# Softmax sums of a causal attention turned on the vector engine instead of sent through DMA, with the first loads in one row

## The chip, the cores and the metric

One core of a Trainium2 chip. The metric is device time in microseconds (us) of one execution. Engines are named as in the profile: PE (TensorE matmul), PEld (its weight load), DVE (VectorE), ACT (ScalarE), POOL (GpSimd), SP (SyncE, which here only issues DMAs).

## The reference

Two stages, both in float32 for the reader, in 16-bit matmuls in the kernel. Attention over B = 8 batches, H = 8 heads, S = 576 queries, D = 64, with 16 beacon keys that every query sees ahead of the causal ones; then an MLP over all 4608 tokens (512 to 2048 to 512) with a quick-GELU gate:

```python
scores = scale * np.matmul(q, concat(beacon_k, k).T)      # 576 x 592
scores = np.where(causal, -1e9, scores)
a = np.exp(scores - scores.max(-1)); a /= a.sum(-1) + 1e-09
x = np.matmul(a, concat(beacon_v, v))                     # then heads side by side: 4608 x 512
h = x @ w_in
out = (h / (1 + np.exp(-1.702 * h))) @ w_out
```

## The kernel before, in words

**Steps.** The attention runs in 32 steps, one for each batch b and pair of heads p (step i = 4b + p). A step computes the scores of both heads in four chunks (L352, PE, into `s`, two PSUM buffers), exponentiates each (L365, ACT, into `E`), masks the triangles on the diagonal in place (L381 on DVE with a mask tile `keep`, or L388 on POOL), and multiplies with v (L422, PE). v stands in a tile `vb` beside 64 columns of ones, so that the output `u` of a head x and half of the queries (128 rows x 288 columns, one PSUM buffer) holds the unnormalised result in 64 rows and the softmax sum, repeated, in the other 64. For x = 0 the result is in rows 0 to 63, for x = 1 in rows 64 to 127. 18 matmuls of L422 make the four outputs of a step.

**PSUM.** `u` is a ring of four buffers which everything else shares: the turned q, k and v of the first two batches (L178, L215), the L422 outputs, and both MLP layers. PE waits when the fourth buffer back has not been read.

**Normalising.** Each `u` is copied whole to an SBUF tile `O` (L436, an eviction, on ACT or DVE). Two pairs (half a batch, hf) share one `O`. In batches 2 to 7 the sums of two pairs are gathered by two DMAs into a small tile `zc`, DVE takes the reciprocal (`rc`, L455), a DMA writes it to DRAM (`zd`), two DMAs spread it over 64 partitions each (`rz`, 288 KB), and four multiplications of 64 rows (a norm, L500, on DVE or POOL) write `xT`, the MLP's input. In batches 0 and 1 (`TZ = 2`) no DMA is used: DVE transposes the 32 x 32 squares of the sums from `O` (`zt`, L478), takes the reciprocal of one column in 32 (`rt`, L486), and transposes that back, repeated 32 times (`rz`, L491).

**MLP.** Nine groups of 512 tokens; for each, 16 first-layer units (L528, 4 matmuls of 512 columns; tanh on ACT, L539; gate on DVE, L544, into `g`) and four second-layer units (L559, 16 matmuls; halved on ACT or DVE, L570; stored by SP). An L528 unit needs the norms of its batches, so the MLP runs beside later attention steps, and the rest behind the last.

**q and k.** The first two batches come in by POOL's DMAs (L150, L160) and are turned on PE; later batches are loaded to `n` (L132), turned by DVE in squares (L276), reordered by DVE or POOL (L285), written to DRAM and placed (SP).

**What sets the order.** Every piece of work is entered in a list as a `Work` with an engine (or a choice of engines), an estimated duration, a key (a due time in steps) and what it needs. A planner, `issue()`, goes through the list once while the program is built: it takes what could start first, by its estimates, and among those the smallest key. The order that comes out is fixed on each engine; at run time each engine follows its row and waits by semaphores. `MLP0` and `PACE` set the keys of the MLP units. A DMA issued by POOL waits for the one eight issues earlier (`DMASW0` to `DMASW7` are these eight lanes).

Of the kernel before, what the change touches and what calls it, by code (L numbers as in the profile page):

```python
# [10 lines left out]
F32 = mybir.dt.float32  # L11
AFT = mybir.ActivationFunctionType
ALU = mybir.AluOpType
# [3 lines left out]
def kernel(  # L17
# [37 lines left out]
    MLP0, PACE = 6.5, 7  # L55
    FILL, FILLT = 150, 60.0
    VMASK = 8
    TZ = 2
# [7 lines left out]
    op_ = ctx.enter_context(tc.tile_pool(name="op", bufs=2))  # L66
# [363 lines left out]
    def av_out(i, x, half, eng):  # L430
        b, p = divmod(i, NPAIR)
        if (b, p // 2) not in Os:
            Os[(b, p // 2)] = [
                op_.tile([P, 2, S], F32, tag=f"O{y}", name=f"O{y}") for y in range(2)
            ]
        copy[eng](  # L436
            out=Os[(b, p // 2)][x][:, p % 2, half * HS : (half + 1) * HS],
            in_=avu[(i, x, half)][:, :],
        )

# [3 lines left out]
    def z_gather(b, hf, y):  # L444
        if y == 0:
            zst[(b, hf)] = [zp.tile([64, 36], F32, tag="zc", name="zc")]
        src = (Os[(b, hf)][0][D : D + 1, :, :], Os[(b, hf)][1][0:1, :, :])[y]
        nc.sync.dma_start(
            out=zst[(b, hf)][0][32 * y : 32 * y + 32, :],
            in_=src.rearrange("o a s -> o (a s)"),  # L450
        )

    def z_recip(b, hf):
        rc = zp.tile([64, 36], F32, tag="rc", name="rc")
        nc.vector.reciprocal(out=rc[:, :], in_=zst[(b, hf)][0][:, :])  # L455
        zst[(b, hf)].append(rc)

    def z_write(b, hf):
        zd = dr.tile([2, 2 * S], F32, tag="zd", name="zd")
        nc.sync.dma_start(out=zd.rearrange("y (r c) -> (y r) c", c=36), in_=zst[(b, hf)][1][:, :])  # L460
        zst[(b, hf)].append(zd)

    def z_spread(b, hf, y):
        if y == 0:
            zst[(b, hf)].append(zp.tile([P, 2, S], F32, tag="rz", name="rz"))
        nc.sync.dma_start(  # L466
            out=zst[(b, hf)][3][64 * y : 64 * y + 64, :, :].rearrange("r a s -> r (a s)"),
            in_=zst[(b, hf)][2][y : y + 1, :].to_broadcast([64, 2 * S]),
        )

    zts = {}

    def z_turn(b, hf, a, y):
        if (a, y) == (0, 0):
            zts[(b, hf)] = zp.tile([P, 2, TPP, SQ], F32, tag="zt", name="zt", bufs=1)
        nc.vector.transpose(  # L478
            zts[(b, hf)][64 * y : 64 * y + 64, a, :, :],
            Os[(b, hf)][y][64 * (1 - y) : 64 * (1 - y) + 64, a, :],  # L480
        )

    def z_turn_recip(b, hf, a):
        if a == 0:
            zst[(b, hf)] = [None, None, zp.tile([P, 2, TPP], F32, tag="rt", name="rt", bufs=1)]
        nc.vector.reciprocal(out=zst[(b, hf)][2][:, a, :], in_=zts[(b, hf)][:, a, :, 0])  # L486

    def z_turn_back(b, hf, a):
        if a == 0:
            zst[(b, hf)].append(zp.tile([P, 2, S], F32, tag="rz", name="rz"))  # L490
        nc.vector.transpose(  # L491
            zst[(b, hf)][3][:, a, :],
            zst[(b, hf)][2][:, a, :].unsqueeze(2).to_broadcast([P, TPP, SQ]),
        )

    def norm(b, hf, n, eng):
        c = (b % RING) * S
        a, y = divmod(n, 2)
        r = 64 * y
        vec[eng].tensor_tensor(  # L500
            out=xT[r : r + 64, 2 * hf + a, c : c + S],
            in0=Os[(b, hf)][y][r : r + 64, a, :],
            in1=zst[(b, hf)][3][r : r + 64, a, :],
            op=ALU.mult,
        )
# [88 lines left out]
    class Buf:  # L594
# [5 lines left out]
        n0=2, n1=2, sq=2, t0=2, t1=2, d0=4, d1=4, qT=2, kT=2, vb=2, s=2, E=2, u=4, O=2,  # L600
        zc=2, rc=2, zd=4, rz=2, zt=1, rt=1, xT=RING, sig=3, g=2, osb=3,
# [15 lines left out]
    last = []  # L617

    def first_loads(b):
        k0 = 4 * b - 3  # L620
        gb6 = Buf("g")
        lds = {}
        for g in range(2):
            for w in (1, 0):
                lds[(g, w)] = Work(
                    "POOL", 0.9, k0 - 2 + 0.1 * g, lambda b=b, g=g, w=w: load_qk6(b, g, w),
                    last[:], alloc=gb6 if not lds else None, dma=1.8, after=list(lds.values())[:1],
                )
# [126 lines left out]
    for i in range(NSTEP):  # L755
# [33 lines left out]
        if p % 2 == 0:  # L789
            Ob = Buf("O")  # L790
            evs = {}
        for x in range(2):
            for half in range(2):
# [12 lines left out]
                ev = Work(  # L806
                    dict(DVE=0.44, ACT=0.45), 0, i + 0.5,
                    lambda eng, i=i, x=x, half=half: av_out(i, x, half, eng), [av],
                    alloc=Ob if not evs else None, after=list(evs.values())[:1],
                )  # L810
                use(u_, ev)
                evs[(p, x, half)] = ev
        if b < TZ:
            if p % 2 == 0:
                zb = [Buf("zt"), Buf("rt"), Buf("rz")]
            a = p % 2
            zn = []
            for y in range(2):
                zn.append(Work(
                    "DVE", 0.68, i + 0.45, lambda b=b, hf=hf, a=a, y=y: z_turn(b, hf, a, y),  # L820
                    [e for (pp, x, half), e in evs.items() if (pp, x) == (p, y)],
                    alloc=zb[0] if (a, y) == (0, 0) else None, after=zn[:1],
                ))
            zr = Work(
                "DVE", 0.2, i + 0.45, lambda b=b, hf=hf, a=a: z_turn_recip(b, hf, a), zn,
                alloc=zb[1] if a == 0 else None,
            )
            zk = Work(
                "DVE", 0.68, i + 0.45, lambda b=b, hf=hf, a=a: z_turn_back(b, hf, a), [zr],
                alloc=zb[2] if a == 0 else None,  # L830
            )
            use(zb[0], *zn, zr)
            use(zb[1], zr, zk)
            use(Ob, *zn)
            for y in range(2):
                n = 2 * a + y
                nw = Work(
                    dict(DVE=0.76, POOL=1.42), 0, i + 0.45,
                    lambda eng, b=b, hf=hf, n=n: norm(b, hf, n, eng), [zk],
                    alloc=xTb[b] if (hf, n) == (0, 0) else None,  # L840
                    after=[norms[(b, 0, 0)]] if (hf, n) != (0, 0) else (),
                )
                norms[(b, hf, n)] = nw
                use(Ob, nw)
                use(zb[2], nw)
# [189 lines left out]
```

## Time and profile before

| | us |
|---|---|
| median of 3 runs | 435.76 (432.81 to 437.97) |
| the profiled execution | 430.96 |
| its span in the profile | 429.1 |
| PE busy | 381.3 (89%) |
| DVE busy | 262.5 (61%) |
| ACT busy | 235.0 (55%) |
| POOL busy | 170.3 (40%) |

The profile is of one execution; its span is what the trace covers, and the 1.9 us beside it lie around the program. A busy PE need not be a fast one: the granted clock (PEclk, 1.00 is full) halves in some stretches. A row of the view of waits names the instruction that waited, then what released it, with the total, the number of times and the longest. In a row of the timeline the bracket holds the idle time ahead of the instruction and what ended it.

### The profile page before, as it was taken

To read this page: it belongs to the slowest core of one execution; us is meant where nothing else is said; L and a number is where in the kernel's file an instruction comes from. 1 tells how busy PE (TensorE), PEld (TensorE's weight loads), DVE (VectorE), ACT (ScalarE), POOL (GpSimd) and SP (SyncE) were. 2 spreads that over 40 slices of the span, in tenths; PEclk is the share of its full clock that TensorE was granted. 3 is DMA by queue.
4 is the path that set the end of the run, shared out by engine and by line. 5 is a ranking of instruction groups with operands and counts; after the bars stand their busy time and mean duration, and the time that the engine had idled before them with its cause. 6 is when DMAs were issued, how large, how long until landed. Compare 5 with 4: busy or idle time off the path is not lost. (4 is left out here: it accounts for less than half of the span.)

```text
span 429.1 us, 6682 instructions
## 1 busy us (share of the span) xinstructions
PE 381.3 (89%) x2459; PEld 188.6 (44%) x2459; DVE 262.5 (61%) x441; ACT 235.0 (55%) x391; POOL 170.3 (40%) x253
## 2 busy tenths in 40 slices
PE   7997777989885988897969898949999999999996
PEld 3454433444442434343434565624445444444442
DVE  5479989699466296826877499353664544534310
ACT  1787766767452458544826666625666353444411
POOL 6458755376246255644438268132332010000000
PEclk9999969899997999698999999979999999999999
DMA  9899996696679727895449759732202031010111
GB/s 119 116 152 200 172 198 123 165 83 157 162 179 165 196 79 177 83 158 156 116 134 145 186 119 151 160 98 80 81 28 82 26 105 49 24 49 26 50 50 73
DMA packets 64929, 50.13 MB, mean 117 GB/s; under 512 B 34689, under 2 KB 55681, under 8 KB 64897
## 3 DMA queue, kind: packets, MB, share of 16 engines
q0 software_dynamic: 42816, 18.62, 38.3%
q1 hardware_dynamic: 22080, 31.10, 24.0%
q8 instruction: 19, 0.31, 0.3%
q14 instruction: 14, 0.11, 0.1%
HBM read 51.48 MB, written 16.72 MB: 159 GB/s over the span
## 5 line engine op out<-in xcount | busy, mean ns | idle before, releaser
L528 PE MATMUL u<-xT,w 128*128 128x512 f16 (+1 forms) x640 | 145.9, 375 | 17.7 <-DVE xT L500 8.3
L559 PE MATMUL u<-w,g 128*128 128x512 f16 x576 | 132.3, 385 | 4.3 <-DVE O L436 4.3
L544 DVE SCALAR_TENSOR_TENSOR g<-sig,u 128x512 f16<-128x512 f16 x144 | 96.1, 679 | 59.0 <-ACT sig L539 57.7
L539 ACT ACTIVATE sig<-u 128x512 f16<-128x512 f32 x144 | 85.9, 602 | 53.3 <-PE u L528 48.7
L365 ACT ACTIVATE E<-s 128x1024 f16<-128x1024 f32 (+3 forms) x128 | 107.0, 872 | 6.5 <-PE s L352 4.0
L528 PEld LDWEIGHTS <-w 128*128 128x128 f16 x640 | 61.0, 101 | 82.5 <-issue 24.8
L388 POOL TENSOR_SCALAR_AFFINE_SELECT E<-E 128x256 f16<-128x256 f16 (+2 forms) x120 | 52.3, 448 | 108.0 <-ACT E L365 106.4
L559 PEld LDWEIGHTS <-g 128*128 128x128 f16 x576 | 56.1, 99 | 72.4 <-issue 9.0
L570 ACT ACTIVATE osb<-u 128x512 f32<-128x512 f32 x36 | 21.5, 597 | 104.0 <-PE u L559 104.0
L422 PE MATMUL u<-E,vb 128*128 128x288 f16 (+6 forms) x576 | 61.0, 248 | 4.3 <-DVE g L544 3.0
L422 PEld LDWEIGHTS <-vb 128*128 128x128 f16 (+1 forms) x576 | 45.0, 99 | 26.3 <-issue 13.3
L500 DVE TENSOR_TENSOR xT<-O,rz 64x576 f16<-64x576 f32 x48 | 45.0, 953 | 18.8 <-DMA rz<-zd 18.4
L352 PE MATMUL s<-qT,kT 64*128 64x80 f16 (+5 forms) x384 | 38.3, 290 | 14.3 <-ACT E L365 6.2
L436 DVE COPY O<-u 128x288 f32<-128x288 f32 x63 | 27.2, 446 | 31.4 <-PE u L422 29.1
L285 POOL COPY t<-sq 128x576 f16<-128x576 f16 x25 | 32.6, 1312 | 31.2 <-DVE sq L276 31.2
L276 DVE STREAM_TRANSPOSE sq<-n 128x576 f16<-128x576 f16 x48 | 34.7, 750 | 7.8 <-DMA n<-in_k_dram 7.7
L500 POOL TENSOR_TENSOR xT<-O,rz 64x576 f16<-64x576 f32 x16 | 25.9, 1619 | 33.3 <-DMA rz<-zd 31.9
L436 ACT COPY O<-u 128x288 f32<-128x288 f32 x65 | 25.2, 404 | 14.8 <-PE u L422 12.4
L352 PEld LDWEIGHTS <-kT 64*128 64x128 f16 x384 | 13.6, 95 | 38.3 <-issue 30.8
L244 POOL DMA_DIRECT2D vb<-in_v_dram x24 | 20.7, 867 | 0.1
L285 DVE COPY t<-sq 128x576 f16<-128x576 f16 x23 | 17.2, 760 | 0.2
L381 DVE TENSOR_TENSOR E<-E,keep 128x256 f16<-128x256 f16 (+2 forms) x40 | 13.6, 366 | 4.9 <-ACT E L365 3.1
(48 smaller groups left out, 135.5 us busy)
## 6 DMA issues: line engine op xcount, KB each, us to landing
out_dram<-osb SPq DMA_DIRECT2D x36, 256.0 KB
rz<-zd SPq DMA_DIRECT2D x24, 288.0 KB
d<-t SPq DMA_DIRECT2D x24, 148.0 KB
kT<-d SPq DMA_DIRECT2D x12, 296.0 KB
n<-in_k_dram POOLq DMA_DIRECT2D x12, 288.0 KB, 6.9
n<-in_q_dram POOLq DMA_DIRECT2D x12, 288.0 KB, 8.1
d<-t SPq DMA_DIRECT2D x24, 144.0 KB
qT<-d SPq DMA_DIRECT2D x12, 288.0 KB
```

The source lines that it names most:

```text
L276: nc.vector.transpose(sqs[(b, g, w)][:, c * n : (c + 1) * n, :, :], nat[(b, g, w)][:, c * n : (c + 1) * n, :],)
L285: copy[eng](out=tqk[(b, g, w)][:, e, o : o + S].rearrange("p (r t) -> p r t", t=TPP), in_=sqs[(b, g, w)][:, :, e, :].rearrange("p t r -> p ...
L352: nc.tensor.matmul(sc[:, x, o : o + e - a], kT[r : r + 64, p, j * P : (j + 1) * P], qT[r : r + 64, p, a:e], start=True, stop=True,)
L365: nc.scalar.activation(out=Es[i][:, :, choff[ci] : choff[ci] + w], in_=scs[(i, ci)][:, :, 0:w], func=AFT.Exp, scale=0.125,)
L388: nc.gpsimd.affine_select(out=blk, in_=blk, compare_op=ALU.is_ge, fill=0.0, base=mc, pattern=[[0, 2], [1, w]], channel_multiplier=-1,)
L422: nc.tensor.matmul(u[:, lo:hi], vb[0:kw, j, :, :].rearrange("r h c -> r (h c)")[:, o : o + 2 * D], E[0:kw, x, col : col + hi - lo], start= ...
L436: copy[eng](out=Os[(b, p // 2)][x][:, p % 2, half * HS : (half + 1) * HS], in_=avu[(i, x, half)][:, :],)
L500: vec[eng].tensor_tensor(out=xT[r : r + 64, 2 * hf + a, c : c + S], in0=Os[(b, hf)][y][r : r + 64, a, :], in1=zst[(b, hf)][3][r : r + 64, ...
L528: nc.tensor.matmul(u[:, o : o + w], w1t[:, kp, nt * P : (nt + 1) * P], xT[:, kp, m : m + w], start=(kp == 0), stop=(kp == NKP - 1),)
L539: nc.scalar.activation(out=sig[:, :], in_=hu[(g, nt)][:, :], func=AFT.Tanh, scale=0.851)
L544: nc.vector.scalar_tensor_tensor(out=gts[g][:, nt, :], in0=hs[(g, nt)][:, :], scalar=1.0, in1=hu[(g, nt)][:, :], op0=ALU.add, op1=ALU.mult,)
L559: nc.tensor.matmul(o[:, :], gts[g][:, nt, mt * P : (mt + 1) * P], w2t[:, nt, :], start=(nt == 0), stop=(nt == NNT - 1),)
```

## The change

All batches now normalise without DMA, one pair at a time. For each of the four `u` of a step DVE transposes the squares of the 64 rows of sums straight out of PSUM (`z_turn`, 64 x 288), and only the other 64 rows are evicted (`av_out`). When the four turns of a pair are there, one reciprocal, one turn back and one multiplication of 128 rows follow. `O` now holds one pair, in three buffers. The planner may give the multiplication to POOL, but the order has all 32 on DVE. `MLP0` is 4.6 for 6.5. The loads of batch 1, and `w_in`, no longer need the v load before them, their due times are all ahead of the first step, and the `w_out` quarters need less.

```diff
-    MLP0, PACE = 6.5, 7
+    MLP0, PACE = 4.6, 7
-    TZ = 2
-    op_ = ctx.enter_context(tc.tile_pool(name="op", bufs=2))
+    op_ = ctx.enter_context(tc.tile_pool(name="op", bufs=3))
...
     def av_out(i, x, half, eng):
+        if i not in Os:
+            Os[i] = op_.tile([P, S], F32, tag="O", name="O")
+        r = 64 * x
+        copy[eng](
+            out=Os[i][r : r + 64, half * HS : (half + 1) * HS],
+            in_=avu[(i, x, half)][r : r + 64, :],
+        )
+    def z_turn(i, x, half):
+        if i not in zst:
+            zst[i] = [zp.tile([P, TPP, SQ], F32, tag="zt", name="zt")]
+        n = HS // SQ
+        nc.vector.transpose(
+            zst[i][0][64 * x : 64 * x + 64, half * n : (half + 1) * n, :],
+            avu[(i, x, half)][64 * (1 - x) : 64 * (1 - x) + 64, :],
+        )
+    def z_recip(i):
+        zst[i].append(zp.tile([P, TPP], F32, tag="rt", name="rt"))
+        nc.vector.reciprocal(out=zst[i][1][:, :], in_=zst[i][0][:, :, 0])
+    def z_back(i):
+        zst[i].append(zp.tile([P, S], F32, tag="rz", name="rz"))
+        nc.vector.transpose(
+            zst[i][2][:, :],
+            zst[i][1][:, :].unsqueeze(2).to_broadcast([P, TPP, SQ]),
+        )
+    def norm(i, eng):
+        b, p = divmod(i, NPAIR)
         c = (b % RING) * S
         vec[eng].tensor_tensor(
+            out=xT[:, p, c : c + S], in0=Os[i][:, :], in1=zst[i][2][:, :], op=ALU.mult
         )
...
     def first_loads(b):
-        k0 = 4 * b - 3
+        k0 = 4 * b
+        kl = -5 + 0.4 * b
...
-                    "POOL", 0.9, k0 - 2 + 0.1 * g, lambda b=b, g=g, w=w: load_qk6(b, g, w),
-                    last[:], alloc=gb6 if not lds else None, dma=1.8, after=list(lds.values())[:1],
+                    "POOL", 0.7, kl + 0.1 * g, lambda b=b, g=g, w=w: load_qk6(b, g, w),
+                    alloc=gb6 if not lds else None, dma=1.8, after=list(lds.values())[:1],
...
-        W1.append(Work("POOL", 1.1, 4.1 + 0.01 * c, lambda c=c: load_w1(c), last[:], dma=3.0))
-        W2.append(Work("POOL", 1.1, 4.2 + 0.01 * c, lambda c=c: load_w2(c), vpe[:], dma=3.0))
+        W1.append(Work("POOL", 0.75, -4 + 0.01 * c, lambda c=c: load_w1(c), dma=3.0))
...
+                zn.append(Work(
+                    "DVE", 0.4, i + 0.48, lambda i=i, x=x, half=half: z_turn(i, x, half), [av],
+                    alloc=zb[0] if not zn else None, after=zn[:1],
+                ))
...
+        zr = Work("DVE", 0.2, i + 0.45, lambda i=i: z_recip(i), zn, alloc=zb[1])
+        zk = Work("DVE", 0.75, i + 0.45, lambda i=i: z_back(i), [zr], alloc=zb[2])
+        nw = Work(
+            dict(DVE=0.78, POOL=1.45), 0, i + 0.45, lambda eng, i=i: norm(i, eng), [zk] + evs,
+            alloc=xTb[b] if p == 0 else None, after=[norms[b * NPAIR]] if p else (),
+        )
```

What this does to the order, at three places. The first is DVE's row in the middle of the program, before, around step 16 counted from 0; `rc<-zc` is the reciprocal, `g<-sig,u` a gate, `sq` and `t` the turning of q and k, `O<-u` an eviction, `xT<-O,rz` a norm:

```order
L381 TENSOR_TENSOR E<-E,keep 128x2x128 [waits Activation_49]
L381 TENSOR_TENSOR E<-E,keep 128x2x80
L455 RECIPROCAL rc<-zc 64x36 [waits DMAHW1_49,DMAHW0_49]
L544 SCALAR_TENSOR_TENSOR g<-sig,u 128x512 [waits Activation_49]
L291 STREAM_TRANSPOSE t_2205<-bk 128x2x32
L276 STREAM_TRANSPOSE sq<-n_2116 128x576
L285 COPY t_2299<-sq 128x576 [waits DMAHW6_49,DMAHW5_49,DVE_49]
L436 COPY O_2219<-u 128x288 [waits PE_49] x2
L436 COPY O_2220<-u 128x288 [waits PE_49]
L500 TENSOR_TENSOR xT<-O_1964,rz 64x576 [waits DMAHW0_49]
L500 TENSOR_TENSOR xT<-O_1965,rz 64x576 [waits DMAHW1_49]
L500 TENSOR_TENSOR xT<-O_1965,rz 64x576
```

The same engine at about the same place, with the change; `zt<-u` is a turn out of PSUM, `rz<-rt` the turn back:

```order
L447 STREAM_TRANSPOSE zt<-u 64x288 [waits PE_49] x4
L507 SCALAR_TENSOR_TENSOR g<-sig,u 128x512 [waits Activation_49]
L454 RECIPROCAL rt<-zt 128x18 [waits DVE_49]
L458 STREAM_TRANSPOSE rz<-rt 128x576 [waits DVE_49]
L507 SCALAR_TENSOR_TENSOR g<-sig,u 128x512 [waits Activation_49]
L466 TENSOR_TENSOR xT<-O,rz 128x576 [waits DVE_49]
L507 SCALAR_TENSOR_TENSOR g<-sig,u 128x512 [waits Activation_49] x2
L275 STREAM_TRANSPOSE sq<-n_2473 128x576 [waits DMASW0_49]
L275 STREAM_TRANSPOSE sq<-n_2473 128x576
```

The reciprocal and the norms no longer wait for DMAs of SP (`DMAHW`), and follow the turns of their own pair; before, the norms of steps 14 and 15 stood behind evictions of step 16 and waited there.

The second place is ACT's row around there, before; `E<-s` is an exp, `sig<-u` a tanh:

```order
L436 COPY O_1964<-u 128x288 [waits PE_49]
L539 ACTIVATE sig<-u 128x512 [waits DVE_49]
L539 ACTIVATE sig<-u 128x512 [waits DVE_49,PE_49]
L365 ACTIVATE E<-s 128x2x464 [waits PE_49]
L436 COPY O_1964<-u 128x288 [waits PE_49]
L365 ACTIVATE E<-s 128x2x208
L436 COPY O_1965<-u 128x288 [waits PE_49] x2
```

And with the change:

```order
L502 ACTIVATE sig<-u 128x512 [waits DVE_49,PE_49]
L533 ACTIVATE osb<-u 128x512 [waits DMAHW3_49,PE_49]
L364 ACTIVATE E<-s 128x2x512 [waits PE_49,Pool_49]
L433 COPY O<-u 64x288 [waits DVE_49] x3
L364 ACTIVATE E<-s 128x2x480
```

An eviction used to wait for PE alone; here three wait for DVE's turns of the same `u`. Of ACT's 114 evictions (65 before) 72 stand so; at the other 42 the turn waits for ACT.

The third place is POOL's row at the start, before; `g` are q and k of the first batches, `w_99<-in_v_dram` their v:

```order
L150 DMA g<-in_q_dram 96x4x384
L160 DMA w_99<-in_v_dram 96x8x384
L99 AFFINE_SELECT spread<-spread 96x648 [waits DVE_49]
L87 AFFINE_SELECT keep<-keep 128x144
L388 AFFINE_SELECT E<-E 128x2x112 [waits Activation_49]
L388 AFFINE_SELECT E<-E 128x2x128 [waits Activation_49]
L388 AFFINE_SELECT E<-E 128x2x80
L388 AFFINE_SELECT E<-E 128x2x128 [waits Activation_49] x2
L150 DMA g<-in_k_dram 96x4x384
L150 DMA g<-in_q_dram 96x4x384 [waits DMASW0_49]
```

With the change, from the second load of batch 1 on:

```order
L149 DMA g<-in_q_dram 96x4x384 [waits DMASW0_49]
L149 DMA g<-in_k_dram 96x4x384 [waits DMASW1_49]
L149 DMA g<-in_q_dram 96x4x384 [waits DMASW2_49]
L159 DMA w_99<-in_v_dram 96x8x384 [waits DMASW3_49]
L98 AFFINE_SELECT spread<-spread 96x648 [waits DVE_49]
L250 DMA w_98<-in_moe_w_in_dram 128x4x512 [waits DMASW4_49]
L250 DMA w_98<-in_moe_w_in_dram 128x4x512 [waits DMASW5_49]
L250 DMA w_98<-in_moe_w_in_dram 128x4x512 [waits DMASW6_49]
L250 DMA w_98<-in_moe_w_in_dram 128x4x512 [waits DMASW7_49]
L86 AFFINE_SELECT keep<-keep 128x144
L257 DMA w_99<-in_moe_w_out_dram 128x4x512 [waits DMASW0_49]
L387 AFFINE_SELECT E<-E 128x2x112 [waits Activation_49]
```

The masks of the first step (`E<-E`) moved behind batch 1's loads, all of `w_in` and a quarter of `w_out`; each of these DMAs waits for an earlier one to land before it is issued.

More of the change, by code (lines that the diff above doesn't have):

```diff
@@ L473 @@
[L473 to L486, printed above, removed]
@@ L878 @@
+        norms[i] = nw
+        use(zb[0], zr)
+        use(zb[1], zk)
+        use(zb[2], nw)
+        use(Ob, nw)
     for w, i in late:
```

135 lines of the change are left out of this document (15 added, 120 removed).

## The prediction

> **What bounds the kernel now.** First the page: who is busy, and for how much of the span.
>
> ```profile
> span 429.1 us, 6682 instructions
> PE 381.3 (89%) x2459; PEld 188.6 (44%) x2459; DVE 262.5 (61%) x441; ACT 235.0 (55%) x391; POOL 170.3 (40%) x253
> ```
>
> PE bounds it, but a mean over stages hides where it loses time. I cut the span where a step's last L422 matmul ends (18 a step): step 8 of 32 ends at 82.1, step 32 at 335.7. The view by windows (columns: length, busy time of each engine, granted clock, DMA share, GB/s):
>
> ```profile
> core 0: us, PE busy (x) PEld busy (x) DVE busy (x) ACT busy (x) POOL busy (x), PEclk, DMA share, GB/s
> 10.00:82.10 72.10, 59.33 (x563) 31.80 (x558) 57.24 (x97) 52.30 (x88) 43.12 (x70) 0.93 1.03 160
> 82.10:335.50 253.40, 224.49 (x1456) 113.23 (x1455) 164.89 (x286) 145.74 (x243) 119.36 (x167) 0.95 0.68 129
> 82.10:101.60 19.50, 17.91 (x118) 8.88 (x117) 18.94 (x34) 14.64 (x27) 12.51 (x19) 1.00 0.91 136
> 200.00:220.00 20.00, 19.84 (x127) 9.68 (x126) 16.13 (x28) 13.31 (x23) 9.46 (x13) 0.93 0.42 103
> 335.70:425.60 89.90, 89.81 (x417) 40.51 (x414) 34.40 (x51) 34.85 (x60) 1.39 (x1) 1.00 0.15 51
> ```
>
> The tail after 335.7 is pure matmul at full clock: nothing to win there. The 24 steps of 82.1 to 335.5 lose 253.4 - 224.5 = 28.9 us to waits of PE and, at a mean clock of 0.95, 0.05 x 253.4 = 12.7 us to a slow clock; unhindered they would be 211.8 us. The view of waits says whom PE waited for there:
>
> ```profile
> PE u L528 <- DVE xT L500: 8.3, 5, 5.5
> PE u L528 <- DVE O L436: 5.4, 2, 4.0
> PE u L559 <- DVE O L436: 4.3, 1, 4.3
> PE u L528 <- DVE g L544: 3.4, 3, 2.1
> ...
> DVE xT L500 <- DMA rz<-zd: 18.4, 9, 6.6
> DVE rc L455 <- DMA zc<-O: 11.2, 4, 6.3
> ```
>
> PE names DVE, and DVE, from its own waits, names the two DMAs of the softmax sums. The timeline shows both as one event, and the chain of waits has it at its head too:
>
> ```profile
> 131.04 0.75 DVE L500 TENSOR_TENSOR xT<-O,rz 64x576 f16<-64x576 f32 x1 [2.77 <-DMA rz<-zd]
> 135.06 1.47 DVE L436 COPY O<-u 128x288 f32<-128x288 f32 x4
> 135.50 1.01 PE L559 MATMUL u<-w,g 128*128 128x512 f16 x2 [4.32 <-DVE O L436]
> 172.97 1.44 PE L528 MATMUL u<-xT,w 128*128 128x512 f16 x3 [2.07 <-DVE g L544]
> 275.41 8.34 DMA rz<-zd
> ```
>
> DVE stood at a norm (L500) whose broadcast had not landed; the evictions behind it in DVE's queue (L436) came late, and PE, which needed a `u` buffer that one of them held, stood 4.32 us. So DVE, idle in a third of these steps, bounds PE by what it waits for. Behind such waits the clock drops; the seventh number is the clock:
>
> ```profile
> 134.60:141.40 6.80, 5.90 (x14) 2.02 (x14) 3.97 (x9) 0.00 (x0) 3.60 (x6) 0.50 1.11 143
> 172.20:178.90 6.70, 5.93 (x17) 2.06 (x16) 5.84 (x9) 1.75 (x5) 4.24 (x6) 0.50 0.31 66
> ```
>
> Each wait thus costs itself and half of some 6.8 us. The Trainium skill (TensorE: Matmul & The Clock Gate, HAM oscillation) asks for no idle gap over about 3.4 us; the trace is stricter, since the 2.07 us at 172.97 stood at a half clock as well. By that rule only waits over 3.4 us would carry the surcharge, and a crowd of new waits of 1 us would cost no more than their own length.
>
> **The change part by part.**
>
> *The chain of sums without DMA.* Per pair of heads: four turns out of PSUM, one reciprocal, one turn back, one norm of 128 rows. In the 24 steps the DMA waits go, and PE's 8.3 + 5.4 + 4.3 with them, and the 3.4 of gates that stood behind norms: 21.4 us, and the 12.7 us of clock. On SP 60 issues go (24 zc, 12 zd, 24 rz), which the writes of q and k no longer queue behind. Late next is DVE itself, for the work moves there. Its rows, and one of ACT, from the 24 steps (count, busy us, mean ns, idle before), and from L478 on from the whole run:
>
> ```profile
> L500 DVE TENSOR_TENSOR xT<-O,rz 64x576 f16<-64x576 f32 x31 | 29.7, 977 | 18.7 <-DMA rz<-zd 18.4
> L436 DVE COPY O<-u 128x288 f32<-128x288 f32 x54 | 23.3, 447 | 28.7 <-PE u L422 26.6 <-issue 1.8
> L455 DVE RECIPROCAL rc<-zc 64x36 f32<-64x36 f32 x11 | 4.0, 363 | 11.2 <-DMA zc<-O 11.2
> L381 DVE TENSOR_TENSOR E<-E,keep 128x256 f16<-128x256 f16 x17 | 6.2, 367 | 1.1 <-ACT E L365 1.0
> L276 DVE STREAM_TRANSPOSE sq<-n 128x576 f16<-128x576 f16 x40 | 28.9, 749 | 7.7 <-DMA n<-in_k_dram 7.7
> ...
> L436 ACT COPY O<-u 128x288 f32<-128x288 f32 x41 | 15.9, 404 | 8.6 <-PE u L422 6.4 <-POOL xT L500 1.2 <-POOL E L388 0.7
> L478 DVE STREAM_TRANSPOSE zt<-O 64x576 f32<-64x576 f32 x16 | 12.4, 773 | 2.6 <-ACT O L436 2.1
> L491 DVE STREAM_TRANSPOSE rz<-rt 128x576 f32<-128x576 f32 x8 | 6.2, 769 | 0.1
> L486 DVE RECIPROCAL rt<-zt 128x18 f32<-128x18 f32 x8 | 2.0, 247 | 0.0
> L500 DVE TENSOR_TENSOR xT<-O,rz x48: 718/756/1907, 29.5 to 355.7; 64x576 f16<-64x576 f32 x48
> ```
>
> Added: 96 turns out of PSUM, a form that no trace shows. A copy of the same 288 columns out of PSUM takes 0.447 (L436), a turn of 576 columns from SBUF 0.773 (L478). Ends: 0.39, half of 0.773, if all of a turn goes by columns, and 0.773 if none does; I take 0.47, close to the copy, which shares source and length. 96 x 0.47 = 45.1 (37.4 to 74.2). 24 reciprocals x 0.247 = 5.9. 24 turns back x 0.769 = 18.5. 24 norms, twice the rows but the same 576 columns, now all on DVE: 0.82, between the median 0.756 and the mean 0.977, since POOL's norms go: 19.7. Together 89.2. Gates, by the order, 92 for 89: +2.0. Removed: 29.7; 23.3 less 12 evictions that stay (5.4); 4.0; 17 masks that the order gives to POOL (17 x 0.37 = 6.3); 5 turns of q and k that it puts ahead of step 8 (3.7): 61.6. DVE goes from 164.9 to 194.5 us (187 to 224). Against the 211.8 us of PE that is 92%: **DVE becomes nearly as full as PE.**
>
> The longest norm took 1907 ns, and POOL gets 143 masks for 120. The Trainium skill (SBUF — State Buffer, Who interferes with whom) says that a DVE instruction with two SBUF inputs, as a norm is, contends with POOL instructions that read SBUF, and one with at most one such input does not. By that rule norms stay at the mean of 0.977, and DVE's sum is 24 x 0.157 = 3.8 us higher, 400 in place of 396 below if all of it reached PE; the turns out of PSUM are spared. By the rows it lies between.
>
> *What that does to PE* the windows show. With DVE at 81% (16.13 of 20) PE was busy 19.84 of 20. With DVE at 97% (18.94 of 19.5) PE was 8% idle. I take 7% on 211.8: 226 us, where DVE stands at 86%, between these rows. Ends: none (212), and 17% (248), twice the 8% of the fuller row, when the turn is at its high end (DVE 224 us, 90% of 248).
>
> *A wait added.* In the order an ACT eviction of `u` waits for the DVE turn of the same buffer, or the turn for the eviction. Queued behind such an eviction on ACT are exps and tanhs, for which PE and DVE wait. ACT has room: 145.7 of 253.4 us busy, and some 41 evictions more at 0.404 make 162. Where four turns stand in a row with the evictions after them, ACT lags by one of them a step, which the 7% holds; what it costs when PE pays for every one is a rival below.
>
> *The loads in one row.* POOL issues 12 loads before `spread`, then `w_in` and one `w_out` load, and the first masks stand behind all.
>
> ```profile
> 4.89 0.67 POOL L150 DMA_DIRECT2D g<-in_q_dram  x1
> 5.55 0.78 POOL L160 DMA_DIRECT2D w<-in_v_dram  x1
> 12.82 0.38 POOL L388 TENSOR_SCALAR_AFFINE_SELECT E<-E 128x224 f16<-128x224 f16 x1 [5.50 <-ACT E L365]
> 16.33 6.65 PE L215 MATMUL u<-w,spread 96*128 96x512 f16 x30
> 23.68 1.75 PE L422 MATMUL u<-E,vb 128*128 128x288 f16 x18
> g<-in_q_dram POOLq DMA_DIRECT2D x4, 288.0 KB, 6.2
> w<-in_v_dram POOLq DMA_DIRECT2D x2, 576.0 KB, 9.2
> ```
>
> Its last lane waits for batch 1's first q load. The last q of batch 0 (4.89 + 6.2) landed at about 11.1, v behind it (5.55 + 9.2) at about 14.8, so 576 KB took some 3.7 us; k and q of batch 1, 288 KB each, land as much later, near 18.5; three masks like this one end at about 20. PE needs them at 23.68: its 6.65 us of v matmuls hide the delay, and I cost it at nothing; without that cover it is up to 7 us, the shift of the masks. What arrives earlier (batch 1, `w_in`) nobody waited for by the rows above, so no gain either.
>
> *More MLP earlier.* Counted in the order, steps 1 to 8 get 3 more L528 groups and 2 of L559: 9.5 us of PE work that leaves the tail, where 37 and 14 groups stay of 44 and 15.
>
> ```profile
> L559 PE MATMUL u<-w,g 128*128 128x512 f16 x240 | 53.4, 379 | 0.0
> L528 PE MATMUL u<-xT,w 128*128 128x512 f16 x176 | 39.6, 379 | 0.0
> ```
>
> The tail's 59 groups of 89.9 us are 15 x 16 + 44 x 4 = 416 matmuls of 0.216; 372 remain: 80.4 us. In the first stretch PE had 72.1 - 59.3 = 12.8 us idle and 0.07 x 72.1 = 5 us of clock, and DVE's work is about the same, so most of the 9.5 us fits: I put step 8's end at 84, 91 if none of it is hidden, 79 if a quarter of the idle time goes as well.
>
> *Sum:* 84 + 226 + 80.4 + 3.6 (end of the tail to the end of the span) + 1.9 (430.96 - 429.1) = **396 us**. The profiled execution lies 1.1% under the median of the runs; that share would make it 400. Fewer waits leave less to differ between runs, so I say 398.
>
> **The rivals.**
>
> *All waits vanish:* DVE's slack suffices: 79 + 212 + 80.4 + 5.5 = 377. For it: the 19.84 of 20 above. Against: DVE was at 81% there, not 92%. 15%.
>
> *DVE takes DMA's place:* 91 + 248 + 80.4 + 5.5 = 425, if the turn is nearer 0.77 us or the in-order queue of a full DVE holds `u` too long. For it: 97% of DVE with PE 8% idle after 82.1. Against: a copy of that length takes 0.447. 16%.
>
> *The two reads of `u` come one after the other on PE's path (slower):* 128 buffers held 0.45 us longer; with all four taken, PE waits each time: 57.6 us, and the 12.7 of slow clock return, on 82 + 211.8 + 80.4 + 5.5 = 379.7: 450. It decides once new waits pass 51 us. For it: the 4.32 us wait had this cause. Against: four buffers and three engines below 90%. 5%.
>
> *The sums' DMA was hidden anyway:* 431, no change: only if other waits filled its place at once; PE's waits name it too plainly. 4%.
>
> **How the numbers follow.** Forecast 60% (388 to 412). The range takes in the first two rivals to beyond their centres, 377 to 428; the slower rival, no change and about a third of each other rival stay out, 2 in 10. A measurement of this kernel tells about 1% from no change. Faster by more (under 431.4): 0.60 + 0.15 + 0.13 of the second = 0.88. Within: 0.04 + 0.02 = 0.06. Slower: 0.05 + 0.01 = 0.06.
>
> **What would show it.** In the new profile: no row waits for rz<-zd or zc<-O; the turn's row near 0.47; DVE over 80% from step 8 to 32; PE's waits under 20 us there, named to DVE turns and gates, none over 3 us; half clock in fewer than three stretches; PE full from about 310. Wrong would make it: turns near 0.77, ACT evictions waiting long for DVE, or masks after 23 us at the start.

## The result, and the profile after

The changed kernel takes **403.6 us** (median of 4 runs, 402.97 to 404.79); the kernel before, on the same chip, 434.28 us (432.08 to 437.97). The ratio is 0.9289 with a 95% interval of 0.9213 to 0.9364: faster, by 31 us of medians. 398 was forecast, 377 to 428 the range. The profiled execution took 404.15 us.

The page of the profile after, span and busy times:

```profile
span 402.4 us, 6639 instructions
PE 370.1 (92%) x2458; PEld 187.0 (46%) x2458; DVE 282.2 (70%) x501; ACT 254.5 (63%) x439; POOL 150.7 (37%) x261
```

PE has the same work; it lost part of its idle time and most of its slow clock. A step's last attention matmul is now L421: step 8 ends at 83.3, step 32 at 318.2. The windows cut there (columns as before):

```profile
10.00:83.30 73.30, 65.91 (x592) 34.96 (x586) 57.98 (x106) 56.00 (x96) 40.27 (x71) 0.98 1.07 158
83.30:318.20 234.90, 216.48 (x1459) 112.76 (x1458) 189.99 (x345) 165.95 (x291) 101.60 (x174) 0.99 0.62 112
318.20:398.50 80.30, 80.28 (x372) 36.18 (x370) 28.14 (x43) 30.60 (x52) 0.00 (x0) 1.00 0.12 43
```

The 24 steps went from 253.4 to 234.9 us, the tail from 89.9 to 80.3, the start from 82.1 to 83.3. In the 24 steps PE is idle for 234.90 - 216.48 = 18.4 us (28.9 before), and the clock of 0.99 costs some 2 us (12.7 before). The view of waits in these steps (total, times, longest), some of PE's rows first, then some of DVE's:

```profile
PE u L421 <- DVE g L507: 6.0, 7, 2.4
PE s L351 <- ACT E L364: 4.0, 6, 1.6
PE u L491 <- ACT O L433: 2.8, 5, 1.0
PE u L491 <- DVE g L507: 2.4, 3, 1.9
...
DVE zt L447 <- PE u L421: 17.6, 11, 4.1
DVE sq L275 <- DMA n<-in_k_dram: 10.0, 5, 5.4
...
DVE sq L275 <- DMA n<-in_q_dram: 2.0, 3, 0.9
```

No row names a DMA of the sums: they are gone. PE's longest wait is 2.4 us. What DVE waits for among DMAs is now the loads of q and k (L275 turns them), 12.0 us in all; before it was 7.7 for k's. These loads did not land sooner for the lighter DMA: 7.2 and 8.7 us from issue (median, k and q) where it was 6.9 and 8.1. The groups of DVE in the 24 steps give the price of the new work:

```profile
L447 DVE STREAM_TRANSPOSE zt<-u 64x288 f32<-64x288 f32 x97 | 44.2, 471 | 23.0 <-PE u L421 17.6 <-ACT O L433 3.4
L275 DVE STREAM_TRANSPOSE sq<-n 128x576 f16<-128x576 f16 x36 | 26.5, 754 | 12.1 <-DMA n<-in_k_dram 10.0 <-DMA n<-in_q_dram 2.0
L458 DVE STREAM_TRANSPOSE rz<-rt 128x576 f32<-128x576 f32 x24 | 18.4, 768 | 0.4
L466 DVE TENSOR_TENSOR xT<-O,rz 128x576 f16<-128x576 f32 x24 | 18.1, 756 | 0.9
L454 DVE RECIPROCAL rt<-zt 128x18 f32<-128x18 f32 x24 | 6.2, 260 | 0.4
```

A turn of 288 columns out of PSUM takes 471 ns, hardly more than the copy of before (447). The largest stop that is left, in the timeline, and the landing time of these loads from the view of DMAs (KB each, median us from issue):

```profile
113.55 0.78 DVE L275 STREAM_TRANSPOSE sq<-n 128x576 f16<-128x576 f16 x1 [5.41 <-DMA n<-in_k_dram]
114.91 0.65 DVE L507 SCALAR_TENSOR_TENSOR g<-sig,u 128x512 f16<-128x512 f16 x1
115.61 0.40 PE L421 MATMUL u<-E,vb 128*128 128x288 f16 x3 [2.40 <-DVE g L507]
n<-in_k_dram POOLq DMA_DIRECT2D x12, 288.0 KB, 7.2
n<-in_q_dram POOLq DMA_DIRECT2D x12, 288.0 KB, 8.7
```

It is the old event with another DMA at its head: DVE stood 5.41 us at a turn of k that had not landed, the gate behind it came late, and PE, which needed the gate's `u`, stood 2.40 us. The planner had counted on 5.4 us from the start of an issue to the landing, at the least (0.9 for the issue, 0.7 and 1.8 for the transfer, 2 behind it), for a load that takes 7.2 or 8.7. The half clock is left in two places, where seven were before (the timeline's row ahead of one, and the windows of both):

```profile
32.00 1.01 PE L351 MATMUL s<-qT,kT 64*128 64x512 f16 x8 [2.24 <-ACT E L364]
32.00:35.40 3.40, 3.40 (x24) 2.19 (x24) 2.70 (x5) 2.60 (x5) 1.18 (x3) 0.50 1.24 205
117.40:120.80 3.40, 3.13 (x17) 1.53 (x15) 3.31 (x8) 2.51 (x5) 2.63 (x4) 0.50 0.00 0
```

The longest single waits of PE ahead of the two are 2.24 and 2.40 us, as one of 2.07 was before. The Trainium skill (TensorE: Matmul & The Clock Gate, HAM oscillation) puts the gap at about 3.4 us; this trace disagrees with it again. The length of one wait does not decide it either: behind waits of 1.80 us (to 62.94) and 1.88 us (to 139.00) the clock stayed full here, behind one of 1.82 us (to 56.75) in the kernel before it halved. In the 3.40 us up to the end of the wait PE had been busy for 1.60 and 1.52 us in the first two, for 0.67 us in the third and for 0.76 us ahead of 32.00. That is no rule: in e7 below, behind a wait of 1.79 us (to 63.70) with 1.60 us busy, the clock was 0.61 in the next 3.40 us. What sets it these runs do not show.

### The profile page after: what moved, and what is told of

Read it like the earlier page. It is cut to its first block, busy times and chain, and to the rows that moved or that the text cites. A ratio compares the mean times of both kernels' runs of the same rounds, so it can differ in the third digit from the quotient of the medians.

```text
span 402.4 us, 6639 instructions
## 1 busy us (share of the span) xinstructions
PE 370.1 (92%) x2458; PEld 187.0 (46%) x2458; DVE 282.2 (70%) x501; ACT 254.5 (63%) x439; POOL 150.7 (37%) x261
## 4 chain that ended last, share of the span: by engine, by line
PE 39%; DVE 8%; DMA 4%; ACT 2%; issue 1%; POOL 1%; SPq 0%; DVEq 0%; ACTq 0%
PE u L522 19%; PE u L491 14%; PE u L421 4%; DMA d<-t 2%; DMA n<-in_q_dram 2%; DVE zt L447 2%; DVE g L507 2%; DVE sq L275 2%; PE s L351 2%; DVE t L284 1%; ACT O L433 1%; DVE rz L458 1%; POOL t L284 1%; ACT E L364 1%; DVE xT L466 0%
## 5 line engine op out<-in xcount | busy, mean ns | idle before, releaser
L491 PE MATMUL u<-xT,w 128*128 128x512 f16 (+1 forms) x640 | 138.1, 358 | 7.0 <-ACT O L433 3.5
L522 PE MATMUL u<-w,g 128*128 128x512 f16 x576 | 130.1, 380 | 0.3 <-DVE O L433 0.3
L387 POOL TENSOR_SCALAR_AFFINE_SELECT E<-E 128x256 f16<-128x256 f16 (+2 forms) x143 | 57.8, 418 | 109.3 <-ACT E L364 107.0
L502 ACT ACTIVATE sig<-u 128x512 f16<-128x512 f32 x144 | 84.3, 601 | 21.9 <-PE u L491 16.4
L491 PEld LDWEIGHTS <-w 128*128 128x128 f16 x640 | 58.5, 97 | 65.2 <-issue 15.2
L447 DVE STREAM_TRANSPOSE zt<-u 64x288 f32<-64x288 f32 x128 | 58.4, 472 | 25.9 <-PE u L421 18.5
L421 PE MATMUL u<-E,vb 128*128 128x288 f16 (+6 forms) x576 | 60.6, 248 | 10.2 <-DVE g L507 7.8
L433 ACT COPY O<-u 64x288 f32<-64x288 f32 x114 | 43.6, 392 | 29.1 <-DVE zt L447 19.7
L421 PEld LDWEIGHTS <-vb 128*128 128x128 f16 (+1 forms) x576 | 46.5, 99 | 31.4 <-issue 12.8
L275 DVE STREAM_TRANSPOSE sq<-n 128x576 f16<-128x576 f16 x48 | 35.4, 753 | 12.1 <-DMA n<-in_k_dram 10.0
L466 DVE TENSOR_TENSOR xT<-O,rz 128x576 f16<-128x576 f32 x32 | 24.6, 769 | 1.1
L458 DVE STREAM_TRANSPOSE rz<-rt 128x576 f32<-128x576 f32 x32 | 24.6, 768 | 0.6
L214 PE MATMUL u<-w,spread 96*128 96x512 f16 x60 | 13.6, 379 | 0.0
```

Source lines behind the costliest of these rows:

```text
L275: nc.vector.transpose(sqs[(b, g, w)][:, c * n : (c + 1) * n, :, :], nat[(b, g, w)][:, c * n : (c + 1) * n, :],)
L387: nc.gpsimd.affine_select(out=blk, in_=blk, compare_op=ALU.is_ge, fill=0.0, base=mc, pattern=[[0, 2], [1, w]], channel_multiplier=-1,)
L421: nc.tensor.matmul(u[:, lo:hi], vb[0:kw, j, :, :].rearrange("r h c -> r (h c)")[:, o : o + 2 * D], E[0:kw, x, col : col + hi - lo], start= ...
L433: copy[eng](out=Os[i][r : r + 64, half * HS : (half + 1) * HS], in_=avu[(i, x, half)][r : r + 64, :],)
L447: nc.vector.transpose(zst[i][0][64 * x : 64 * x + 64, half * n : (half + 1) * n, :], avu[(i, x, half)][64 * (1 - x) : 64 * (1 - x) + 64, :],)
L491: nc.tensor.matmul(u[:, o : o + w], w1t[:, kp, nt * P : (nt + 1) * P], xT[:, kp, m : m + w], start=(kp == 0), stop=(kp == NKP - 1),)
```

## The experiments

All times in one table: the median, its ratio to the kernel before on the same chip with the interval, then of the profiled execution the end of step 8, the length of the 24 steps, and the rest of the span. The four groups (1 to 4, 5 to 8, 9 to 12, and the kernel after) ran on different occasions; the median of before was 431.6, 432.6, 431.8 and 434.3 us in them, so small differences between groups are read from the ratios. e6_light and e8_turn_const leave a part of the work out, so their outputs are not the reference's.

| kernel | median us | ratio | step 8 ends | 24 steps | rest |
|---|---|---|---|---|---|
| before | 434.28 | 1 | 82.1 | 253.4 | 93.4 |
| after | 403.60 | 0.9289 (0.9213 to 0.9364) | 83.3 | 234.9 | 84.2 |
| e1_squares | 410.90 | 0.9537 (0.9490 to 0.9584) | 82.7 | 233.1 | 93.6 |
| e2_sums_alone | 412.31 | 0.9576 (0.9504 to 0.9648) | 88.3 | 228.8 | 93.7 |
| e3_loads_mlp | 432.34 | 1.0020 (0.9986 to 1.0054) | 75.9 | 270.9 | 83.9 |
| e4_squares_loads_mlp | 402.01 | 0.9334 (0.9285 to 0.9382) | 76.1 | 240.2 | 84.2 |
| e5_landing | 394.28 | 0.9125 (0.9079 to 0.9171) | 85.7 | 225.0 | 84.2 |
| e6_light | 400.58 | 0.9277 (0.9218 to 0.9335) | 83.7 | 231.5 | 84.2 |
| e7_heavy | 412.56 | 0.9552 (0.9499 to 0.9605) | 85.3 | 239.8 | 84.2 |
| e8_turn_const | 396.10 | 0.9168 (0.9116 to 0.9221) | 79.5 | 230.2 | 84.2 |
| e9_squares_landing | 393.15 | 0.9119 (0.9081 to 0.9157) | 76.2 | 230.8 | 84.2 |
| e10_serial_landing | 391.91 | 0.9087 (0.9026 to 0.9147) | 78.2 | 226.1 | 84.9 |
| e11_before_landing | 428.64 | 0.9937 (0.9905 to 0.9969) | 86.3 | 250.1 | 93.5 |
| e12_serial | 398.12 | 0.9238 (0.9191 to 0.9284) | 78.0 | 232.5 | 84.9 |

The first eight steps do not hold the same work everywhere: 52 or 53 MLP matmuls in before, e1, e2 and e11, 80 or 81 in e3, e4, e9, e10 and e12, 96 in the kernel after and e5 to e8. Sixteen of them, one second-layer unit, take 3.5 us at the tail's 0.216 each, and what is not in these steps is in the 24 or in the rest.

### Which part of the change is the gain

**e1_squares**, the kernel before with DVE's squares in all batches, turned from the evicted tile `O` in SBUF, half a batch at a time:

```diff
-    TZ = 2
+    TZ = 8
```

> The kernel before with TZ = 8 for 2: the sums of all batches turned by DVE from the evicted SBUF tile, half a batch at a time, no DMA; loads and MLP0 as before. My theory (the DMA of the sums was what PE waited for): faster than before, but less than the change, since a turn of 576 columns from SBUF costs 0.773 us twice a pair and each norm has 64 rows: DVE 164.9 + 24 x (2 x 0.773 + 0.247 + 0.769) - 4 = 222 us in the 24 steps, more than PE's 211.8; with DVE at 90% they take 246, and 82 + 246 + 89.9 + 5.5 = 423 us (410 to 428). Rival (the loads in one row and the earlier MLP bring the gain): no change, 430 to 436.

**e2_sums_alone**, the changed kernel with the loads and the MLP's start of before:

```diff
-    MLP0, PACE = 4.6, 7
+    MLP0, PACE = 6.5, 7
...
-        k0 = 4 * b
-        kl = -5 + 0.4 * b
+        k0 = 4 * b - 3
...
-                    "POOL", 0.7, kl + 0.1 * g, lambda b=b, g=g, w=w: load_qk6(b, g, w),
-                    alloc=gb6 if not lds else None, dma=1.8, after=list(lds.values())[:1],
+                    "POOL", 0.9, k0 - 2 + 0.1 * g, lambda b=b, g=g, w=w: load_qk6(b, g, w),
+                    last[:], alloc=gb6 if not lds else None, dma=1.8, after=list(lds.values())[:1],
...
```

> The kernel after with the loads and MLP0 of before: only the sums are changed. My theory: nearly all of the gain stays; step 8 ends near 80, the 24 steps take the 235 us that they take after, the tail is 89.9 again: 405 to 413 us. Rival (loads and earlier MLP): near before, 428 to 436.

**e3_loads_mlp**, the other half alone: the kernel before, DMA sums and all, with the new loads and `MLP0`:

```diff
-    MLP0, PACE = 6.5, 7
+    MLP0, PACE = 4.6, 7
...
-        k0 = 4 * b - 3
+        k0 = 4 * b
+        kl = -5 + 0.4 * b
...
-        W1.append(Work("POOL", 1.1, 4.1 + 0.01 * c, lambda c=c: load_w1(c), last[:], dma=3.0))
+        W1.append(Work("POOL", 0.75, -4 + 0.01 * c, lambda c=c: load_w1(c), dma=3.0))
...
```

> The kernel before with the loads in one row and MLP0 = 4.6; the sums go by DMA as before. My theory: PE still waits for rz<-zd, so the time stays within 1.5% of before, 428 to 440 us. Rival: most of the gain, 403 to 412 us.

**e4_squares_loads_mlp**, e1 and e3 together: everything in the change but the turn straight out of PSUM and the work by pairs.

> e1_squares with the loads in one row and MLP0 = 4.6: the change but for the turn straight out of PSUM and the norm of a whole pair. My theory: DVE, with two turns of 0.773 us and two norms of 64 rows a pair, holds it above the change: 410 to 422 us. Rival (no DMA and the early MLP are all of it, the way of turning is nothing): 401 to 407 us.

Taking the sums off the DMA is worth 18 to 20 us alone (ratios 0.9576 and 0.9537). The loads and the earlier MLP alone are worth nothing (1.0020), yet about 9 us on top of the new sums (0.9576 to 0.9289, and 0.9537 to 0.9334). The two are not additive, and e3 shows where the sum goes. The window of its 24 steps, and its first row of PE's waits:

```profile
75.90:346.80 270.90, 226.83 (x1478) 116.55 (x1476) 177.56 (x304) 149.78 (x241) 122.69 (x173) 0.92 0.64 126
PE u L528 <- DVE O L436: 24.7, 4, 10.8
```

Its first steps are 6 us shorter and its tail 9.5, but PE stands 44 us in between, at a clock of 0.92 (3.5 of the 17.5 us by which these steps are longer are one MLP unit more): what was gained at both ends is waited away, most of it at DVE's evictions, while DVE itself waits 39.0 us for the sums' DMA there (29.6 before). With the sums off the DMA the ends keep their gain, less some 6 us (228.8 to 234.9 in the 24 steps).

e1 was expected at 423 us, from how full DVE would be; it took 410.9, at the lower edge of what was given, with DVE busy for 216.6 of 233.1 us (93%) and PE idle for 19.1. e4, too, was expected higher, at 410 to 422; it took 402.0, where its rival stood.

How the squares are turned is worth nothing that shows: 402.0 from SBUF (e4), 403.6 out of PSUM, with ratios inside each other's intervals. The rows of e4 say what it does instead (its 24 steps, its turn of 576 columns and its norm of 64 rows in the whole run):

```profile
76.10:316.30 240.20, 222.11 (x1477) 114.78 (x1476) 218.77 (x357) 152.66 (x259) 132.83 (x186) 0.98 0.63 114
L478 DVE STREAM_TRANSPOSE zt<-O 64x576 f32<-64x576 f32 x64 | 49.5, 773 | 2.4 <-ACT O L436 0.4
L500 DVE TENSOR_TENSOR xT<-O,rz 64x576 f16<-64x576 f32 x43 | 49.6, 1153 | 0.4
```

DVE is 91% busy there (218.77 of 240.20), 81% in the kernel after, and PE is idle for the same 18 us in both. That is against the prediction's rule that PE's idle time follows DVE's share, and the next four runs went for it.

### What makes the idle time that is left

Two theories stood: DVE's fullness (PE's waits rise and fall with DVE's work), and single stops in DVE's queue (late loads, one reader of `u` behind another).

**e5_landing**, the changed kernel with a longer landing time in the planner, nothing else; with the rest of its estimate a load now counts 9.4 us from the start of its issue, for 5.4, which is a margin over the 7.2 and 8.7 of the trace. The planner then sets a new order for all engines:

```diff
-                w.t1 = dma_free[eng] + (1.0 if t < 12 else dict(SP=4.0, POOL=2.0)[eng])
+                w.t1 = dma_free[eng] + (1.0 if t < 12 else dict(SP=4.0, POOL=6.0)[eng])
```

> The kernel after, with one number of the planner changed: it takes 6 us for the landing of POOL's loads where it took 2 (the trace has 7.2 and 8.7 us from issue to landing), so the turns of q and k stand later in DVE's row. DVE stood 12 us at turns of q and k whose load had not landed, and 5.4 us of it made PE wait 3.3. Theory that such stops in DVE's queue are what is left: PE's 18.4 us of waits in the 24 steps fall by 5 or more, 394 to 400 us. Rival (DVE is full, and where it stops does not matter): 401 to 406.

Its 24 steps, its group of turns of q and k there, the landing times that it then had, and PE's waits for gates in these steps:

```profile
85.70:310.70 225.00, 215.72 (x1461) 112.46 (x1462) 191.38 (x346) 166.63 (x291) 104.47 (x178) 0.99 0.67 118
L275 DVE STREAM_TRANSPOSE sq<-n 128x576 f16<-128x576 f16 x37 | 27.5, 752 | 0.2
n<-in_k_dram POOLq DMA_DIRECT2D x12, 288.0 KB, 4.4
n<-in_q_dram POOLq DMA_DIRECT2D x12, 288.0 KB, 6.4
PE u L491 <- DVE g L507: 0.4, 1, 0.4
PE u L421 <- DVE g L507: 0.3, 1, 0.3
```

The 12.1 us ahead of the turns are 0.2, PE's idle time 9.3 us for 18.4, PE's waits for gates 0.7 for 8.4, the 24 steps 9.9 us shorter, with the work of DVE and PE as it was. Since the turns stand later and the loads also land sooner, the run does not tell which of the two emptied the row. The gain is all in these steps; the first eight are 2.4 us longer, at a clock of 0.93 for 0.98. By medians it is 9.3 us, by ratios 1.6 points, some 7 us.

**e6_light** leaves out the 32 reciprocals and turns back; the norm multiplies by a constant tile, so the output is not divided by the sums:

```diff
-            out=xT[:, p, c : c + S], in0=Os[i][:, :], in1=zst[i][2][:, :], op=ALU.mult
+            out=xT[:, p, c : c + S], in0=Os[i][:, :], in1=one[:, :], op=ALU.mult
```

> The kernel after, in the same order, without the 32 reciprocals and 32 turns back (the norm multiplies by a constant tile, so the division by the sum is left out): 32 x (0.26 + 0.77) = 33 us less on DVE, all four turns and their waits kept. Theory that the fullness of DVE sets PE's waits (as predicted): waits fall by more than half, 391 to 396 us. Rival (the waits are of single stops in the order, not of DVE's load): 399 to 405.

**e7_heavy** makes every turn back twice, the second time into a tile that nobody reads:

```diff
+        more = zp.tile([P, S], F32, tag="more", name="more")
+        nc.vector.transpose(
+            more[:, :],
+            zst[i][1][:, :].unsqueeze(2).to_broadcast([P, TPP, SQ]),
+        )
```

> The kernel after, in the same order, with each turn back made twice, the second into a tile that nobody reads: 32 x 0.77 = 24.6 us more on DVE, which would be busy 208 of 235 us in the 24 steps. Theory that DVE's fullness sets PE's waits: 412 to 425 us. Rival (single stops): under 410, since a DVE at 91% in the run with the turns from SBUF had PE waiting no longer than the change has.

The 24 steps of both, light first:

```profile
83.70:315.20 231.50, 217.54 (x1461) 112.86 (x1460) 170.04 (x297) 165.68 (x291) 102.71 (x174) 0.99 0.63 114
85.30:325.10 239.80, 219.68 (x1459) 114.02 (x1460) 203.30 (x373) 166.22 (x291) 102.71 (x174) 0.98 0.61 111
```

20.0 us less of DVE work there (170.04 for 189.99) brought 3.4, 13.3 us more cost 4.9. Over the whole run the heavy kernel costs 9.0 us by medians for 16.7 us more of DVE's busy time. So a fuller DVE costs PE something, a sixth of the work in one direction and a third to a half in the other, and the heavy run, 412.56, is at the lower edge of what the fullness theory had said and over the 410 of single stops. The light run is where single stops had put it. But an emptier one gives nearly nothing back: DVE at 73% still has PE idle for 14.0 us. Fullness alone does not make the 18.4.

**e8_turn_const** lets the turn read a constant tile in SBUF, so that it waits neither for L421 nor for the eviction of the same `u`; the sums of the softmax are left out:

```diff
-            avu[(i, x, half)][64 * (1 - x) : 64 * (1 - x) + 64, :],
+            one[64 * (1 - x) : 64 * (1 - x) + 64, 0:HS],
```

> The kernel after, in the same order, with the turn reading a constant SBUF tile in place of u (the sums are left out): DVE's work is the same, but an eviction no longer waits for a turn or a turn for an eviction, and u is free after one read. Theory that the two reads one after the other cost the 9 us that the 24 steps took over the forecast: 392 to 397 us. Rival (the four buffers hide it): 400 to 405.

```profile
79.50:309.70 230.20, 216.37 (x1459) 112.47 (x1460) 188.66 (x347) 164.05 (x290) 101.58 (x174) 0.99 0.64 115
```

By medians 7.5 us less than the kernel after, by ratios 1.2 points, with intervals that just overlap. 3.8 us of it come in the first eight steps, 4.7 in the 24. DVE's waits for loads are still there (14.2 us). The run bounds what the two reads of one `u` in a row cost, but not sharply, since the edit also frees DVE of its own wait for L421. The Trainium skill (PSUM — Partial Sum Buffer, PSUM bank collisions raise a hardware error) reports that two engines may read different 32-partition quadrants of one bank at once; the sums and the result stand in different ones here, and the program makes the second reader wait all the same. No run here had both reads at once, so this stays untried.

### Telling the planner

The last four tell the planner of one wait or of both. **e9_squares_landing** is e4 with the landing time of e5; **e11_before_landing** is the kernel before with it; **e12_serial** is the changed kernel with one more need, that an eviction comes after the turn of the same half, **e10_serial_landing** has that need and the landing time:

```diff
-                    lambda eng, i=i, x=x, half=half: av_out(i, x, half, eng), [av],
+                    lambda eng, i=i, x=x, half=half: av_out(i, x, half, eng), [av, zn[-1]],
```

> The kernel before with the sums' transpose by vector squares from the evicted tile in SBUF, no DMA of sums, the early loads and the earlier MLP (which gave 402.0), and the planner's landing time of POOL's loads raised from 2 to 6 us. If single stops in VectorE's queue behind late loads make what is left of TensorE's waits, they go here as they went in the changed kernel (403.6 to 394.3): 391 to 397. If the gain there hung on the turn out of PSUM (its plan happened to fall better), nothing moves or it gets worse: 400 to 408.

> The changed kernel with two numbers of the planner made true to the trace: POOL's loads land after 6 us instead of 2, and the eviction of a half of u may start only when the turn of the same half is done (as it goes on the chip). If the 7.5 us that a turn from a constant tile saved come from a plan that does not know of the second wait, a plan that knows gets some of them back: 387 to 393. If the chain of two reads costs as much however it is planned, 393 to 397, as with the landing time alone.

> The kernel before, with its DMA of the sums, with the landing time of POOL's loads raised from 2 to 6 us and nothing else. If the landing time is a gain of its own, beside the sums: 420 to 427 (431 to 434 less 7 to 11). If the sums' DMA is the wait that ends last, so that the loads' stops are hidden behind it, as the early loads and the earlier MLP were: 428 to 436.

> The changed kernel with the planner told only that the eviction of a half of u comes after its turn (landing time 2 us, as it was). If the plan's ignorance of the second wait is what costs 7.5 us: 396 to 400. If the chain costs as much however it is planned: 401 to 407.

The windows of the 24 steps in the order 9, 10, 11, 12:

```profile
76.20:307.00 230.80, 216.97 (x1477) 113.27 (x1476) 212.06 (x343) 153.06 (x260) 141.70 (x200) 1.00 0.65 119
78.20:304.30 226.10, 217.74 (x1476) 113.80 (x1475) 205.43 (x376) 158.49 (x270) 102.96 (x177) 1.00 0.64 118
86.30:336.40 250.10, 222.34 (x1457) 113.72 (x1456) 173.93 (x289) 145.62 (x244) 114.38 (x167) 0.95 0.69 133
78.00:310.50 232.50, 219.76 (x1477) 113.75 (x1477) 202.44 (x377) 161.22 (x274) 105.09 (x173) 0.99 0.64 115
```

The landing time works wherever the sums' DMA is gone, with DVE at 92% too (e9: 2.2 points by ratios). The three pairs that differ in it alone (after and e5, e4 and e9, e12 and e10) differ by 9.9, 9.4 and 6.4 us in the 24 steps, each with ratios outside each other's intervals, so it is not the luck of one order. With the DMA in place it is worth 0.6%: DVE's waits for loads vanish there as well, and it stands at the sums instead:

```profile
DVE rc L455 <- DMA zc<-O: 19.4, 6, 8.5
DVE xT L500 <- DMA rz<-zd: 14.0, 5, 7.1
```

That is 33.4 us where it was 29.6. The order of the two reads, told to the planner (e12), gives 398.1 for 403.6. The first eight steps are 5.3 us shorter and the 24 steps 2.4, but one MLP unit of 3.5 us moved from the first to the second: at like work it is some 2 and 6 us. By ratios the intervals overlap, so the gain is likely and not shown. With both (e10) PE is idle for 8.4 us in the 24 steps at full clock, while DVE is at 91% (205.43 of 226.10): 391.9 us, the lowest median of all, and faster than both kernels (0.9087, 0.9026 to 0.9147). From e9 (0.9119) and e5 (0.9125) these runs do not tell it apart.

## Why the prediction was right

Its range held the time and its mechanism is what the runs show; its point was 5.6 us low. The sum for the profiled execution, 396, was 8.2 us low. The 2 us added to it for the difference between executions brought the point nearer by luck, since this time the profiled execution (404.15) was no faster than the median. Step by step:

- **The DMA of the sums is what bounds the kernel.** Right. Without it 18 to 20 us go by that alone (e1, e2), and with it neither earlier loads and MLP (e3) nor better planned ones (e11) show more than 0.6%.
- **The turn at 0.47 us, the reciprocal 0.247, the turn back 0.769, the norm 0.82.** Measured 0.471, 0.260, 0.768 and 0.756; DVE 190.0 us in the 24 steps for 194.5. The lower end, half of the turn from SBUF, and the upper are both out. Norms ran at the old median, not at the mean of 0.977, although POOL has its masks still: the long ones went with POOL's norms. e4 fits with that the other way round, where POOL has 21 norms and DVE's take 1.153.
- **The start, 84, and the tail, 80.4.** 83.3 and 80.3. The masks: `keep`, which POOL makes behind the loads, was ready only at 18.34, and the masks ended at 21.3, under the v matmuls as said:

```profile
16.03 6.65 PE L214 MATMUL u<-w,spread 96*128 96x512 f16 x30
18.02 0.32 POOL L86 TENSOR_SCALAR_AFFINE_SELECT keep<-keep 128x144 f16<-128x144 f16 x1
18.37 0.45 DVE L380 TENSOR_TENSOR E<-E,keep 128x256 f16<-128x256 f16 x2 [4.31 <-POOL keep L86]
19.28 2.06 POOL L387 TENSOR_SCALAR_AFFINE_SELECT E<-E 128x224 f16<-128x224 f16 x6
```

- **The loads bring no gain.** The sum came out right with it, the statement is not shown: with the loads and the earlier MLP the first eight steps end 5 to 7 us earlier (88.3 to 83.3, 82.7 to 76.1, 82.1 to 75.9), although they hold more MLP. Early MLP cannot shorten them, so the loads are the likely reason; no run had one without the other. The prediction asked whom PE waited for among the loads only at the first masks. The view of waits of the kernel before, from 10.00 to 82.10, has PE at the q of the later steps:

```profile
PE s L352 <- DMA qT<-d: 2.6, 1, 2.6
PE s L352 <- DVE qT L186: 1.9, 2, 1.5
PE s L352 <- ACT qT L186: 1.8, 1, 1.8
```

  The first of these is 4.4 us in e1 and 8.7 in e2; in the kernel after it is gone, and the other two are 0.3 each.
- **The 24 steps, 226 us: the term that was mis-sized,** 234.9, by 8.9. Its base was 211.8 and is 214.5 (234.9 less 18.4 idle and 2 of clock). On it the prediction laid 14.2 us, read off two windows as a function of DVE's share; the run has 20.4 of idle time and slow clock. The size was off because the step behind it does not hold: DVE at 81% went with no idle PE in the window of before (a window of 20 us, in which PE ran at a clock of 0.93) and with 8% here, and at 91% with 8% in e4 and 4% in e10. What the 8.9 us are, e5 shows: with a longer landing time in the planner the same work takes 225.0, and e9 and e10 bear it out. The prediction had the row for it (DVE's turns of k waited 7.7 us before) and asked only whether the loads of the start were late, not what would stand at the head of DVE's queue once the sums did not.
- **The added wait.** ACT's evictions waited 14.1 us in 25 times for DVE's turns in the 24 steps; PE paid for few of them. The slower rival, in which it pays for each, is out by a wide margin: e8 bounds the whole cost at about 7.5 us, where that rival had 57.6.
- **What would show it:** waits under 20 us (18.4) and none over 3 (2.4), half clock in under three stretches (two), DVE over 80% (81). PE full from 318 and not from 310. The waits were to name DVE's turns and gates: they name gates (8.4 us), exps (4.0) and ACT's evictions (4.5), a turn in only one wait of 0.4 us.

The edge rivals: all waits gone (377) is not reached even by e10; DVE in DMA's place (425) is not reached by e7 either, with 13.3 us more for DVE in the 24 steps (412.6).

## What to carry to other kernels

When the wait at the head of an in-order queue is taken away, look in the same view for the next one at that head: here it told more of what was left than the engine's busy share did. The edits that bring work forward were worth nothing while such a wait stood, and 9 us once it was gone, so try such edits again after. Where a planner fixes the order, compare its landing times with those of the trace and leave a margin: here that one number was worth 7 to 9 us and the form of the new instructions nothing that showed.

## What the runs showed of the hardware that was not expected

- The turn of 32 x 32 squares out of PSUM costs hardly more than a copy of the same length: 471 ns for 64 x 288 for 447, where a turn of 64 x 576 from SBUF takes 773.
- The 32 added turns of e7 take 23.5 us by their group, but DVE's busy time over the run rose by 16.7 (282.2 to 298.9). Neighbouring DVE instructions overlap in the records, by some 0.07 us at an added turn (one starts at 167.34, takes 0.73 and the next starts at 168.00), which makes some 2 us. Other groups of DVE, the norms above all (23.7 us for 24.6), add up to 2 to 3 us less in that run. The rest is open.

```profile
L463 DVE STREAM_TRANSPOSE more<-rt 128x576 f32<-128x576 f32 x32 | 23.5, 735 | 0.0
PE 374.7 (92%) x2458; PEld 188.5 (46%) x2458; DVE 298.9 (73%) x533; ACT 254.8 (62%) x439; POOL 150.7 (37%) x261
```

- Planned for a longer landing, the same loads also land sooner, 4.4 and 6.4 us for 7.2 and 8.7: they are issued at other times. What else makes them faster was not tried.
